# Moving two of eight streamed value tiles from a dense stage into a softmax wait

## The chip, the core and the metric

The kernel runs on one core of one Trainium2 chip. The metric is the device time of one execution in microseconds (us), the median over runs. Engines are named as in the profile: PE multiplies matrices, PEld is its weight load, DVE is the vector engine, ACT the scalar engine, POOL the general one, SP the queue that issues almost all transfers. Matmuls read SBUF and write PSUM, whose buffers are handed out by pools; a pool with one buffer gives the next tile the same place, so its writer has to wait until the tile before has been read.

## The reference

Two layers, each an attention block and a gated feed-forward block, are applied one after the other to four single-token sequences, with the same weights and the same caches in both layers:

```
def _A_ref(x, k_cache, v_cache, wq, wo):       # Hq 32, Hkv 8, Sk 4096, Dh 128
    q = (x @ wq) per head; k, v = caches, each kv head used by 4 query heads
    p = softmax(q k^T * Dh ** -0.5)
    return (p v) as [B, 1, 4096] @ wo
def _B_ref(x, w_gate, w_up, w_down):           # D 512, F 1792
    return (gelu(x @ w_gate) * (x @ w_up)) @ w_down

x = x + A(layernorm(x)); x = x + B(layernorm(x))
x = x + A(layernorm(x)); x = x + B(layernorm(x))
```

x is [4, 1, 512]; each cache is [4, 8, 4096, 128] in bf16, 32 MB. The caches are most of what has to be read, and the second layer needs them again.

## The kernel before, in words

**Tiling.** Batch b's keys and values are cut into tiles of 512 KB: a kv head has two (`NT` = 2) of 2048 positions each, on 128 partitions with 16 positions apiece. A head group has 4 kv heads (`GH`), so 8 tiles (`TG`); there are two groups. Keys stay in SBUF (`KP`) for both layers. Values go through a ring of 8 slots (`V_SLOTS`, class `VRing`, L607).

**Order of the work.** The order is written by hand: the kernel runs in a manual schedule, so each engine's queue holds its instructions in the order of the Python calls. The main loop runs over b. `attend_first` and the dense stage of b = 0 come first. Then, for each b, the dense stage of layer 1 is followed by the q rows of layer 2 and by `attend(b+1)`, which works on two batches at once: layer 2 of batch b and layer 1 of batch b+1. In `attend(b)`, `gx, gy` are the two groups; the scores of layer 2 (`sc2`) come first, with their softmaxes and the layer-2 values that are still in SBUF (`vals2`), then the scores of layer 1: group `gx`, softmax, group `gy`, softmax. DVE turns each key tile (L488, `turn`) before layer 1's scores use it. `vals1.step(n)` multiplies the next n value tiles. The first group's eight tiles are spent before and just behind the second group's softmax, the second group's eight after it, mixed with the output projection (`rows.heads`). The last three of these are kept in their slots for layer 2, and two are parked in PSUM by DVE (L500) and copied back by ACT later.

**The streamed tiles.** Eight layer-2 value tiles of batch b - 1, those of the group that layer 1 read first (`other2 = order[:TG]`), are loaded a second time. They are held back in `late2`, an object of `Streamed` (L794), which `attend` returns; the dense stage gets it as `prev`. `fill()` takes the next tile: `stream_v` (L692) multiplies it with the probabilities as weights, 8 matmuls of 32 x 256 into a PSUM tile `so`. `whole()` ends a pair of heads: DVE turns `so` (`turn_v`, L700), sums it (L707) and scales it (L708) into `OT2_bf`. In the kernel before, a pair of heads shares one `so` of 512 columns in the pool `ps_sc`, which has one buffer (tag "sc"); the scores use that same buffer, except for the first ones of each `attend`.

**Dense stage** (`dense`, from L1080; for b of 1 to 3 there are streamed tiles, for b = 0 `prev` does nothing). In order: `add_x`, a fill, the statistics, half of the gate matmuls, a fill (`halfway`), the other half; inside `gelu`, `up()` issues the up matmuls and two fills; then `gate_up` (L433), `whole()` for the first pair, the 56 down matmuls (`down_rows`, L273) and two fills. The main loop goes on with the q rows of layer 2, a fill behind `q_round`, a fill behind `q_build`, and `whole()` for the second pair. Eight fills in all.

**What sets the transfers.** SP runs its queue in order. `ring.extend` appends tiles to the ring's sequence; `ring.pump` (L617, the transfer itself L623) issues the next load for each free slot, at the point of the program where it is called. A load waits for the last reader of its slot, and whatever stands behind it on SP waits too. In `attend` the sequence is: `one(b)` (16 layer-1 tiles; for b of 2 and 3 the first two are loaded ahead), the 8 of `other2`, then the 3 of `own1`, which are layer-2 tiles for the next `attend`.

Of the kernel before, what the change touches and what calls it, by code (L numbers as in the profile page):

```python
# [8 lines left out]
FP32 = mybir.dt.float32  # L9
# [6 lines left out]
P = 128  # L16
# [18 lines left out]
def kernel(  # L35
# [15 lines left out]
    _, Hkv, Sk, Dh = A_k_cache.shape  # L51
# [8 lines left out]
    NT = C // CH  # L60
# [6 lines left out]
    TG = GH * NT  # L67
# [480 lines left out]
    def soft_turn(p0):  # L548
        flat = p0[0].rearrange("p c j -> p (c j)")
        nc.vector.transpose(out=flat, in_=flat)  # L550
# [32 lines left out]
    def one(b):  # L583
        return [(g * GH + s, t) for g in first_groups[b] for s in range(GH) for t in range(NT)]
# [113 lines left out]
    def turn_v(ps, n=1):  # L698
        flat = ps[:, :n * SW]
        nc.vector.transpose(out=flat, in_=flat)  # L700

    def sum_v(ps, out, rden, n=1):
        first = ps[:, :1]
        own = bass.AP(first.tensor, first.offset,
                      [list(first.ap[0]), [SW, n], [1, rep], [QS + rep, NW]])
        sums = ov[:, :n * rep].rearrange("p (k h) -> p k h", h=rep)
        nc.vector.tensor_reduce(out=sums, in_=own, axis=AX.X, op=ALU.add)  # L707
        nc.vector.tensor_tensor(out=out.rearrange("p (k h) -> p k h", h=rep), in0=sums, in1=rden,  # L708
                                op=ALU.mult)

    class Values:
# [8 lines left out]
        def fill(self, count):  # L720
            self.step(count, hold=True)
# [72 lines left out]
    class Streamed:  # L794
# [3 lines left out]
            self.b, self.tiles, self.prob, self.dst, self.n = b, tiles, prob, dst, 0  # L798
            self.sums = []

        def fill(self):
            kvh, t = self.tiles[self.n]
            self.n += 1
            g, s = divmod(kvh, GH)
            pe = self.prob[g][0]
            if t == 0 and s % 2 == 0:
                ps = ps_sc.tile([P, 2 * SW], FP32, name="so", tag="sc")
                self.sums.append((kvh, ps))
            ps = self.sums[-1][1]
            ring.pump()  # L810
            v, own = ring.ready.pop((2, self.b, kvh, t))
            at = s % 2 * SW
            stream_v(ps[:, at:at + SW], pe[:, s], v, t, t == 0, t == NT - 1)
            assert own
            ring.free.append(v)
            ring.pump()

        def whole(self):
            kvh, ps = self.sums.pop(0)
            g, s = divmod(kvh, GH)  # L820
            turn_v(ps, 2)
            sum_v(ps, self.dst(kvh, 2), self.prob[g][1][:, s:s + 2], 2)

    def dst1(b):
        last = one(b)[-1][0]
# [94 lines left out]
    def attend(b, qy, before, norm, early=None):  # L920

        gx, gy = second_groups[b - 1]
        prob1, prob2 = {}, {}
        keys, parked = early or (Keys(b, (gx, gy)), None)
        turn = keys.turn
        kept2, own2, other2, apart2 = two(b - 1)
        kept1, own1, _, apart1 = two(b)
        banks.late = len(apart2)
        vals2 = Values(2, b - 1, kept2 + own2 + apart2, prob2, dst2(b - 1),
                       off_ot=len(apart2) > 0)  # L930
        late2 = Streamed(b - 1, other2, prob2, dst2(b - 1))
        vals1 = Values(1, b, one(b), prob1, dst1(b), keeps=kept1,
                       streamed=[gy * GH + s for s in range(GH - 1)], park=apart1,
                       sums={4: (ps_sc, "sc"), 5: (ps_sm, "sm"), 6: (ps_sc, "sc")},
                       last_bank=lambda: ps_sm.tile([P, 2, WIDE], FP32, name="ot", tag="sm"))

        sc2 = [new_scores(early=True)]
        for t in range(NT):
            scores(sc2[0], gx, t)
            if parked and t == 0:  # L940
                freed = KP[gx][0][0]
                home = freed.rearrange("p h c d -> p (h c d)")
                parked.back(home, 2)
                KP[gx][0][0], KP[gy][NT - 1][1] = KP[gy][NT - 1][1], freed
                keys.load_pairs(GH // 2 - 1)
            else:
                keys.load_pairs(GH // 2)
        p0 = soft(sc2[0], norm)
        if parked:
            parked.back(home, 2)  # L950
        q_build(qy())
        sc2.append(new_scores())
        soft_turn(p0)
        ready = 2 if parked else 0
        turn(ready)
        for t in range(NT):
            scores(sc2[1], gy, t)
            keys.load(GH)
        ring.extend(1, b, one(b)[ahead_of[b]:])
        ring.extend(2, b - 1, other2)  # L960
        ring.extend(2, b, own1)
        pe0, den0 = soft_swap(p0, early=True), soft_den(p0)

        def recip():
            prob2[gx] = (pe0, soft_recip(den0))

        p1 = soft(sc2[1], norm, lasting=True, meanwhile=recip)
        vals2.step(2, hold=True)
        qe = q_sums(q1_bf[:, gx, :, b])
        vals2.step(4, hold=True)  # L970
        turn()
        soft_turn(p1)
        q_spread(qe)
        vals2.flush()
        turn(1 if ready else 2)
        pe1, den1 = soft_swap(p1, early=True), soft_den(p1)
        banks.back_brief()
        banks.back()
        turn()
        prob2[gy] = (pe1, soft_recip(den1))  # L980
        turn(0 if ready else 1)
        sc1 = new_scores()
        scores(sc1, gx, 0)
        turn(3)
        scores(sc1, gx, 1)
        turn()
        p0 = soft(sc1)
        vals2.step(vals2.left(), hold=True)
        turn()
        soft_turn(p0)  # L990
        q_build(q1_bf[:, gy, :, b])
        vals2.flush()
        pe, den = soft_swap(p0), soft_den(p0)
        turn()
        prob1[gx] = (pe, soft_recip(den))
        turn()
        vals1.step(2)
        sc1 = new_scores()
        scores(sc1, gy, 0)
        turn(4)  # L1000
        vals1.step(3)
        scores(sc1, gy, 1)
        p0 = soft(sc1)
        vals1.step(3)
        soft_turn(p0)
        heads = pairs(one(b))
        twice = o1(b)
        rows = RowProj(lambda i: twice(i).broadcast_to([P, 2]))
        prob1[gy] = (soft_swap(p0), soft_recip(soft_den(p0)))
        vals1.step(2)  # L1010
        rows.heads(heads[0], hp)
        vals1.step(2)
        rows.heads(heads[1], hp)
        vals1.step(1)
        rows.heads(heads[2], rep)
        vals1.step(1)
        rows.heads(heads[2] + rep, rep)
        rows.split()
        vals1.step(1)
        proj = OutProj(o1(b), 1)  # L1020
        proj.heads(heads[3], rep)
        vals1.step(1)
        assert vals1.left() == 0
        rows.onto(proj)
        proj.n = Hq - rep
        proj.heads(heads[3] + rep, rep)
        return proj.y, late2
# [52 lines left out]
    def dense(b0, nb, y, prev, scr):  # L1080
        first = b0 == 0 and nb == 1
        n = 2 * RUN if first else RUN

        def rhs(k):
            return xb[:, k, :n]

        def into(w_sb, name, halfway):
            if first:
                return ffn_in(rhs, w_sb, name, halfway)
            return ffn_rows(b0, w_sb, name, halfway)  # L1090

        def out_of(i, v):
            if not first:
                return turn_rows(v)
            nc.vector.tensor_scalar(out=cs_f[:, i], in0=v[:, :, B], scalar1=float(D), scalar2=None,
                                    op0=ALU.mult)
            return v[:, :, b0:b0 + nb]

        u = []

        def up():
            if first:
                busy(6)
            u.append(into(wu_sb, "u", None))
            if first:
                busy(4)
            else:
                for _ in range(2):
                    prev.fill()
                u[0] = out_of(1, u[0])  # L1110

        add_x(b0, nb, y)
        prev.fill()
        st = stats(b0, nb)
        add_y(b0, nb, y)
        rstd, mr = ln_scale(nb, st)
        t = [None if first else shifts(scr, mr, i) for i in range(2)]
        g = out_of(0, into(wg_sb, "g", prev.fill))
        sq = gelu(scr, g, shifts(scr, mr, 0) if first else t[0], rstd, up)
        uv = out_of(1, u[0]) if first else u[0]  # L1120
        H_bf = gate_up(scr, sq, uv, shifts(scr, mr, 1) if first else t[1], rstd)
        prev.whole()
        if first:
            y = down(nb, H_bf)
            busy(1)
            return y
        y = down_rows(H_bf)
        for _ in range(2):
            prev.fill()
        return turn_rows(y)  # L1130

    def dense_last(y, full):
# [167 lines left out]
```

## Time and profile before

| | |
|---|---|
| runs (3) | 273.52 us median, 272.98 to 275.62 |
| the profiled execution | 273.24 us, its span 271.5 us |
| PE busy | 180.9 us, 67% of the span, mean granted clock 0.843 |
| DVE busy | 176.3 us, 65% |
| ACT busy | 54.1 us, 20% |
| transfers | 103.08 MB, mean 380 GB/s |
| L488 DVE, turning keys | 74.1 us, 64 of 1208 ns |
| L692 PE, streamed values, 128x256 | 20.1 us in two groups, 400 matmuls |
| L759 PE, other values, 128x32 | 34.9 us, 1120 matmuls |

All durations used below come from the profiled execution, and times such as "125.59" are microseconds from the start of its span. "Busy" is summed over stages with different limits, so it does not tell which engine sets the end: that is read at each seam, from what a waiting instruction waits for. In a row of the timeline the numbers are start and length in us, then engine, line, operation, output<-inputs, shape and count, and in brackets the idle time before it with what ended that time. In a row of the chain of waits they are start, length, and what it was. In a table by stretches, each engine has its busy time with the number of instructions; the last three numbers are PE's granted clock, the share of the DMA engines and GB/s.

### The profile page before, as it was taken

Reading aid. Unit: us, or ns where it says so; the run is one execution under the profiler, and the core shown is the slowest. Engines: PE = TensorE matmul, PEld = TensorE weight load, DVE = VectorE, ACT = ScalarE, POOL = GpSimd, SP = SyncE. Lnnn points to the kernel's source line nnn. Section 1 sums busy time; section 2 is a strip of 40 time slices with the busy share of each in tenths; the row PEclk is TensorE's granted clock in tenths of the full one; section 3 lists DMA queues with packets and bytes.
Section 4 is the critical chain, followed back from the end, with each engine's and each line's share of the span. In section 5 each row is a group of like instructions: output and inputs, shape, how many; then the busy total and the mean of one; then the engine's idle time right before and its main releaser. Section 6 shows DMA issues by size and latency. Waiting matters only on the chain.

```text
span 271.5 us, 8960 instructions
## 1 busy us (share of the span) xinstructions
PE 180.9 (67%) x3982; PEld 110.6 (41%) x3982; DVE 176.3 (65%) x445; ACT 54.1 (20%) x113; POOL 2.7 (1%) x8
## 2 busy tenths in 40 slices
PE   1366254644696956868669458787596596977784
PEld 1313133533363524445327134454262253543463
DVE  3394951131224898875776989667759894877673
ACT  1001001100005402031023520310226102105630
POOL 2000000000000000000000000000000000000001
PEclk9999999555599795779997977799978556799999
DMA  7999999999984999999999999999999999999930
GB/s 250 422 416 421 416 421 416 410 383 406 407 325 147 405 415 419 418 418 416 416 404 407 417 420 417 417 416 388 381 421 418 416 423 414 369 383 378 415 132 3
DMA packets 32286, 103.08 MB, mean 380 GB/s; under 512 B 2676, under 2 KB 8568, under 8 KB 32248
## 3 DMA queue, kind: packets, MB, share of 16 engines
q1 hardware_dynamic: 32224, 102.51, 94.8%
q8 instruction: 31, 0.51, 0.7%
q14 instruction: 7, 0.06, 0.0%
q10 hardware_dynamic: 24, 0.01, 0.0%
HBM read 102.50 MB, written 0.00 MB: 378 GB/s over the span
## 4 chain that ended last, share of the span: by engine, by line
DMA 37%; DVE 28%; PE 23%; SPq 6%; issue 3%; ACT 1%; DVEq 0%
DMA v_t<-in_A_v_cache_dram 18%; DVE kp L488 16%; PE sc L521 10%; DMA kp<-in_A_k_cache_dram 9%; DMA wd_sb<-in_B_w_down_dram 6%; DMA kp<-in_A_v_cache_dram 4%; SPq L143 4%; PE ot L759 3%; PE so L692 2%; DVE pe L530 2%; DVE qb L313 2%; PE y L248 2%; PE q L273 1%; DVE q L280 1%; SPq L144 1%
## 5 line engine op out<-in xcount | busy, mean ns | idle before, releaser
L488 DVE STREAM_TRANSPOSE kp<-kp 128x1024 f32<-128x1024 f32 x64 | 74.1, 1208 | 0.0
L521 PE MATMUL sc<-kp,qb 128*32 128x512 bf16 x512 | 57.9, 492 | 20.7 <-DVE kp L488 15.2
L759 PE MATMUL ot<-pe,v_t 128*128 128x32 bf16 x1120 | 34.9, 182 | 13.0 <-DMA v_t<-in_A_v_cache_dram 11.6
L759 PEld LDWEIGHTS <-v_t 128*128 128x128 bf16 x1120 | 33.2, 101 | 23.8 <-DMA v_t<-in_A_v_cache_dram 13.8
L521 PEld LDWEIGHTS <-qb 128*32 128x32 bf16 x512 | 17.0, 106 | 48.6 <-issue 34.6
L542 ACT ACTIVATE pe<-sc,nl 128x512 bf16<-128x512 f32 x8 | 5.5, 687 | 88.8 <-DVE pe L539 61.8
L572 PE MATMUL x<-pe,ident_bf 128*32 128x128 bf16 x192 | 6.3, 262 | 16.5 <-DVE pe L550 16.5
L530 DVE TENSOR_REDUCE pe<-sc 128x1 f32<-128x512 f32 x12 | 8.3, 690 | 11.8 <-PE sc L521 11.8
L572 PEld LDWEIGHTS <-ident_bf 128*32 128x32 bf16 x256 | 5.9, 109 | 19.5 <-issue 18.2
L692 PE MATMUL so<-v_t,pl 128*32 128x256 bf16 x192 | 9.5, 275 | 3.6 <-DMA v_t<-in_A_v_cache_dram 3.4
L248 PE MATMUL y<-OT_bf,wo_sb 128*128 128x32 bf16 x192 | 7.3, 190 | 6.9 <-DMA wo_sb<-in_A_wo_dram 6.7
L248 PEld LDWEIGHTS <-wo_sb 128*128 128x128 bf16 x256 | 8.5, 102 | 8.1 <-DMA wo_sb<-in_A_wo_dram 7.1
L700 DVE STREAM_TRANSPOSE so<-so 128x256 f32<-128x256 f32 (+1 forms) x19 | 11.1, 583 | 1.0 <-PE so L692 0.9
L692 PE MATMUL so<-v_t,pe 128*32 128x256 bf16 x208 | 10.6, 338 | 1.2 <-ACT pe L575 1.1
L507 ACT COPY v_t<-park 128x1024 bf16<-128x1024 bf16 x12 | 11.3, 1031 | 0.0
L550 DVE STREAM_TRANSPOSE pe<-pe 128x512 bf16<-128x512 bf16 x12 | 8.4, 698 | 4.4 <-ACT pe L542 4.4
L370 DVE TENSOR_TENSOR xb<-XX,y 128x4 bf16<-128x4 f32 (+1 forms) x9 | 1.6, 174 | 14.5 <-PE y L248 14.4
L575 ACT CAST pe<-x 128x512 bf16<-128x512 f32 x12 | 7.0, 586 | 19.0 <-PE x L572 19.0
L605 DVE TENSOR_TENSOR OT_bf<-ot,rden 128x8 bf16<-128x8 f32 (+1 forms) x20 | 3.1, 157 | 10.7 <-PE ot L759 10.5
L351 PE MATMUL yr<-wo_sb,OT_bf 128*2 128x512 bf16 (+1 forms) x96 | 9.8, 478 | 0.1
L248 PE MATMUL q<-xb,wq_sb 128*128 128x5 bf16 (+1 forms) x192 | 5.5, 170 | 6.5 <-DMA wq_sb<-in_A_wq_dram 6.5
L307 PE MATMUL qe<-q_bf,ident_bf 128*32 128x16 bf16 x256 | 4.4, 176 | 8.0 <-DVE q_bf L296 6.1
(142 smaller groups left out, 217.3 us busy)
## 6 DMA issues: line engine op xcount, KB each, us to landing
v_t<-in_A_v_cache_dram SPq DMA_DIRECT2D x97, 512.0 KB, 8.4
kp<-in_A_k_cache_dram SPq DMA_DIRECT2D x40, 512.0 KB, 12.1
kp<-in_A_k_cache_dram SPq DMA_DIRECT2D x12, 1024.0 KB, 7.4
wq_sb<-in_A_wq_dram SPq DMA_DIRECT2D x2, 2048.0 KB, 14.7
wo_sb<-in_A_wo_dram SPq DMA_DIRECT2D x4, 1024.0 KB, 11.6
wq_sb<-in_A_v_cache_dram SPq DMA_DIRECT2D x2, 1024.0 KB, 10.8
wg_sb<-in_B_w_gate_dram SPq DMA_DIRECT2D x1, 1792.0 KB
wu_sb<-in_B_w_up_dram SPq DMA_DIRECT2D x1, 1792.0 KB
```

The costliest lines, as they stand in the source:

```text
L143: dq.dma_start(out=wo_sb[:, i * n:(i + 1) * n], in_=wo_dram[:, i * n:(i + 1) * n])
L248: nc.tensor.matmul(dst, lhsT=lhsT, rhs=rhs, start=first, stop=last, skip_group_check=True)
L351: nc.tensor.matmul(self.rows[j:j + x.shape[1]], lhsT=x, rhs=wo_sb[:, i], start=self.n < QD, stop=True, skip_group_check=True)
L488: nc.vector.transpose(out=words, in_=words)
L507: nc.scalar.copy(out=dst[:, i * n:(i + 1) * n], in_=self.parts[i])
L521: nc.tensor.matmul(sc[s * QS:(s + 1) * QS], lhsT=qb[:, w0:w0 + 2 * W], rhs=kt[:, :, be // 2, :, be % 2], start=(t == 0 and be == 0), stop= ...
L530: nc.vector.tensor_reduce(out=m, in_=sc.rearrange("p c j -> p (c j)"), axis=AX.X, op=ALU.min if norm else ALU.max)
L550: nc.vector.transpose(out=flat, in_=flat)
L572: nc.tensor.matmul(x[a * QS:(a + 1) * QS, s], lhsT=ident_bf[:, s * QS:(s + 1) * QS], rhs=pT[:, a], start=True, stop=True, skip_group_check ...
L692: nc.tensor.matmul(ps[d, :NW * QS], lhsT=x[:, w:w + NW].rearrange("p c h -> p (c h)"), rhs=v[:, i:i + NW, d], start=first and i == 0, stop ...
L700: nc.vector.transpose(out=flat, in_=flat)
L759: nc.tensor.matmul(self.ot[:, s % 2], lhsT=v[:, i, :], rhs=wide(pe[:, s, t * CH + i, :]), start=(done == 0 and i == 0), stop=(done == NT - ...
```

## The change

Two of the eight fills move from the dense stage into `attend`, behind the scores and the softmax of the second group and three value steps. Their head (the first of four) gets a PSUM tile of its own in the pool `ps_h`, and its own `whole()` before the reciprocal of that softmax. The second head now also has a tile of its own, in `ps_sc`; the third and fourth share one, as before. The dense stage loses the fill between the gate matmuls and one of the two behind the down matmuls; the two in `up()` stay. The ring's sequence changes with it: the two tiles are loaded between the layer-1 tiles of the first and of the second group.

```diff
@@ class Streamed
-        def fill(self):
+        def fill(self, early=False):
             kvh, t = self.tiles[self.n]
             self.n += 1
             g, s = divmod(kvh, GH)
             pe = self.prob[g][0]
-            if t == 0 and s % 2 == 0:
-                ps = ps_sc.tile([P, 2 * SW], FP32, name="so", tag="sc")
-                self.sums.append((kvh, ps))
-            ps = self.sums[-1][1]
+            alone = s < 2
+            if t == 0 and (alone or s % 2 == 0):
+                pool, tag = (ps_h, "h") if early else (ps_sc, "sc")
+                n = 1 if alone else 2
+                self.sums.append((kvh, n, pool.tile([P, n * SW], FP32, name="so", tag=tag)))
+            ps = self.sums[-1][2]
             ring.pump()
             v, own = ring.ready.pop((2, self.b, kvh, t))
-            at = s % 2 * SW
+            at = 0 if alone else s % 2 * SW
...
         def whole(self):
-            kvh, ps = self.sums.pop(0)
+            kvh, n, ps = self.sums.pop(0)
             g, s = divmod(kvh, GH)
-            turn_v(ps, 2)
-            sum_v(ps, self.dst(kvh, 2), self.prob[g][1][:, s:s + 2], 2)
+            turn_v(ps, n)
+            sum_v(ps, self.dst(kvh, n), self.prob[g][1][:, s:s + n], n)
@@ attend
-        ring.extend(1, b, one(b)[ahead_of[b]:])
-        ring.extend(2, b - 1, other2)
+        ring.extend(1, b, one(b)[ahead_of[b]:TG])
+        ring.extend(2, b - 1, other2[:NT])
+        ring.extend(1, b, one(b)[TG:])
+        ring.extend(2, b - 1, other2[NT:])
         ring.extend(2, b, own1)
...
         p0 = soft(sc1)
         vals1.step(3)
+        for _ in range(NT):
+            late2.fill(early=True)
         soft_turn(p0)
...
-        prob1[gy] = (soft_swap(p0), soft_recip(soft_den(p0)))
+        swapped, den = soft_swap(p0), soft_den(p0)
+        late2.whole()
+        prob1[gy] = (swapped, soft_recip(den))
@@ dense
-        g = out_of(0, into(wg_sb, "g", prev.fill))
+        g = out_of(0, into(wg_sb, "g", None))
...
         y = down_rows(H_bf)
-        for _ in range(2):
-            prev.fill()
+        prev.fill()
         return turn_rows(y)
```

## The prediction

> Names used here: A0 to A7 and B0 to B7 are the value tiles of layer 1's first and second head group in one attention pass, S0 to S7 the streamed second-layer tiles of `late2`. Pass b (1 to 3) is `attend(b)`; dense stage b follows it. Bm is the start of PE's last tile B7, which opens dense stage b.
>
> **What bounds the kernel now.** First the page: the digits of the DMA engines, the share of their queue, and the chain that ended last.
>
> ```profile
> DMA  7999999999984999999999999999999999999930
> q1 hardware_dynamic: 32224, 102.51, 94.8%
> DMA 37%; DVE 28%; PE 23%; SPq 6%; issue 3%; ACT 1%; DVEq 0%
> ```
>
> The transfers fill the span except for a dip near 82 us (before pass 1, which the edit does not touch). But they hold only 37% of the chain: DVE and PE together hold 51%. So two limits lie close together, and I ask at each seam which one ends last. The chain around dense stage 2 (start, length, what):
>
> ```profile
> 171.61 8.86 DMA v_t<-in_A_v_cache_dram
> 180.47 0.05 issue
> 180.51 0.58 PE ot L759 x16
> ...
> 182.27 6.15 DMA v_t<-in_A_v_cache_dram
> 188.42 0.04 issue
> 188.47 0.40 PE so L692 x8
> 188.87 0.89 PE q L273 x16
> ```
>
> B7 lands and PE starts it; later S5 lands and lets the q rows go, which stand behind S5 in PE's queue. Now the timeline of pass 1's end and dense stage 1:
>
> ```profile
> 118.22 0.41 PE L572 MATMUL x<-pe,ident_bf 128*32 128x128 bf16 x16 [1.86 <-DVE pe L550]
> ...
> 122.32 0.46 DVE L700 STREAM_TRANSPOSE so<-so 128x256 f32<-128x256 f32 x1
> ...
> 122.81 0.19 DVE L707 TENSOR_REDUCE ov<-so 128x4 f32<-128x32 f32 x1
> ...
> 124.34 0.57 PE L759 MATMUL ot<-pe,v_t 128*128 128x32 bf16 x16 [0.63 <-DMA v_t<-in_A_v_cache_dram]
> ...
> 125.59 0.57 PE L759 MATMUL ot<-pe,v_t 128*128 128x32 bf16 x16 [0.18 <-DMA v_t<-in_A_v_cache_dram]
> ...
> 131.53 0.22 DVE L433 TENSOR_TENSOR words<-words 128x56 bf16<-128x56 f32 x1
> 131.66 0.72 DVE L700 STREAM_TRANSPOSE so<-so 128x512 f32<-128x512 f32 x1
> 131.80 0.97 PE L273 MATMUL y<-wd_sb,words 128*32 128x128 bf16 x56 [0.83 <-DVE words L433]
> ```
>
> The first row is the wait that the change fills: PE idle 1.86 us until the softmax is turned. B6 and B7 both wait for their landing, 1.25 us apart: that is the time of one tile in the queue. The down projection starts 0.05 us after DVE's L433 ends (131.75): dense runs on DVE, and streamed tiles lie beside it. Pass 3 ends otherwise, and so does the kernel:
>
> ```profile
> 236.82 0.56 PE L759 MATMUL ot<-pe,v_t 128*128 128x32 bf16 x16
> ...
> 244.84 0.40 PE L692 MATMUL so<-v_t,pl 128*32 128x256 bf16 x8 [0.58 <-DMA v_t<-in_A_v_cache_dram]
> ```
> ```profile
> 261.90 0.57 PE L759 MATMUL ot<-pl,kp 128*128 128x32 bf16 x16 [0.41 <-DMA kp<-in_A_v_cache_dram]
> ```
>
> B7 of pass 3 waits for no DMA, and the kernel's last value tile waits only 0.41 us. From 125.59 on, a delay of the PE and DVE work thus reaches the end nearly whole.
>
> **The change, part by part.** *The queue's order.* S0 and S1 are now loaded ahead of B0. Eight slots rotate, so the first eight loads behind A go out when A0 to A7 are read, as before; the queue is full, and B7 lands two tiles later. Pass 1 waits for the queue at B6 and B7 already, so B1 goes from 125.59 to 128.09: **+2.50**. SP passes nothing else; the next two loads are freed by S0 and S1 themselves, not by parked B tiles, so they go out about 3 us earlier (120.49 before), which gives nothing while the queue is full.
>
> *The two early fills.* 2 x 8 matmuls, 0.40 us a tile at full clock (S rows of dense 1), 0.62 in pass 3 at half clock. PE's last A tile ends at 116.36, 171.48 and 228.11, the turned softmax arrives 1.8 us later: 2 x 0.62 fits. In pass 1, S1 lands only at about 118.1 (B1's old place), so the swap is some 0.3 us late; the 2.5 us of waiting above cover it. Without that cover it would cost 0.3. The small `whole` behind it on DVE (0.46 + 0.19 + 0.16, starts 0.49 and 0.23 apart: 0.88) lies in DVE's 0.82 us wait for `den`: nothing, at most 0.1 before the parks.
>
> *Dense without two fills.* The fill between the gate matmuls goes, but DVE's L390 and its turn of the gate follow the layer norm (128.91) as closely as the gate: nothing. S6 no longer stands ahead of the q rows, and S5, two places nearer its PE use, has landed: in stage 1 PE was ready as xb was (133.35, q at 133.41): nothing; in stage 2 xb is ready at 188.27, q starts 188.68: 0.41 less 0.06 of handover, **-0.35**; in stage 3, 244.51 and 245.06: **-0.49**.
>
> *The wait that the change adds.* Head 1 now has its sums alone, and `up()` still fills twice: S3, which ends head 1, and S4, which opens the pair of heads 2 and 3. That pair takes the same PSUM buffer (`ps_sc`, one buffer, tag "sc") that head 1 still occupies, and head 1 is read only by `whole()`, behind `gate_up` on DVE. The order of instructions shows S4's first weight load waiting on DVE, and the 56 down matmuls behind it in PE's queue. Cost in stage 1: turn starts 131.66, the reduction (last reader) 0.49 later and lasts 0.19: 132.34; PE starts S4 0.06 later (132.40), its eight matmuls give way after 0.35, down starts at 132.75 instead of 131.80: **+0.95**, in each of three stages. DVE is free when down ends, since `whole` has moved ahead of it. Bounds: nothing, if S4 does not wait after all (PE idles 0.83 us there now, and S4 has landed: first rival), and 1.15, if PE also waits for the product behind the reduction; I take 0.95, which the rows give for the last reader.
>
> *What the late fills free.* The load behind S4 goes out at the end of S4: stage 1, 7.25 us after the new B1, 135.34 instead of 133.15; its place at the DMA engines comes near 136.3. With an empty queue (84.19, first pair of keys) the trace's half-microsecond windows show 33, 123, 115 GB/s and only from 86.0 on over 300: 1.8 us to speed. So the queue idles some 0.8 us there, and 0.6 before the load behind S6: 1.4 at most, nothing at least if deeper overlap hides it. I take 1.0, nearer to the row. In pass 2 the two sides then meet: PE could have started B7 at about 180.05 (0.46 of waiting left out), + 2.50 + 0.95 = 183.50; the queue brings it at 180.47 + 2.50 + 1.0 = 183.97. So B2 is 184.0, **+3.5** (183.5 to 184.4).
>
> **Sum.** +3.5 at B2; stage 2 +0.95 - 0.35; pass 3 runs on PE and DVE and hands +4.1 on; stage 3 +0.95 - 0.49; the last 0.41 of waiting absorbs as much. 3.5 + 0.6 + 0.46 - 0.41 = +4.15. On the profiled execution's 273.24 (span 271.5): **277.4**, with the two ends of B2 276.9 and 277.8. The median of the runs, 273.52, is 0.28 above that execution, within its neighbours' spread (272.98 to 275.62).
>
> [...] The two passes differ:
>
> ```profile
> 136.40:180.00 43.60, 31.16 (x618) 18.01 (x619) 35.02 (x73) 11.61 (x23) 0.00 (x0) 0.84 1.03 415
> 191.70:236.80 45.10, 34.17 (x624) 19.16 (x625) 35.24 (x73) 11.61 (x22) 0.00 (x0) 0.70 1.02 409
> ```
>
> The same work took 1.5 us more where the granted clock (third number from the end) was 0.70. The clock was 0.50 at 60 to 64 us with PE busy all the time, and 1.00 at 140 to 142 with PE busy 0.48 of 2 us: in this trace more work does not release it. [...]
>
> **Rivals.**
> - *The bank wait stays off the path* (S4 gets in before `whole`, or down does not queue behind it). Then only the order counts: B1 +2.5, B2 at the queue's 182.97 (+2.46), -0.35, -0.49, -0.41: +1.2, **274.5**. For it: the fills of before lay wholly beside DVE. Against: one PE queue.
> - *Faster: the queue alone sets the end.* Between 188 and 196 and between 234 and 252 us it moves 330 to 390 GB/s instead of 420, together 2.9 us of lost transfer. Loads freed up to 4 us earlier by S0, S1 and the B tiles could close these dips: **270.3**. It decides if PE reaches B7 of pass 3 before its landing even 2.5 us later. Against: there PE waits for nothing now, and at the end only 0.41.
> - *The queue runs dry*: 3 us in each dense stage, twice my upper bound. B2 186.0; pass 3's B7 from the queue at 235.85 + 2.5 + 6.0 = 244.3, +7.5; with +0.46 and -0.41: **280.8**. Against: keys and loads have 5 to 10 us of lead after each stage.
> [...]
>
> **How the numbers follow.** My forecast 0.64; bank wait hidden 0.12; faster 0.04; queue dry 0.10; clock released 0.10. The range takes in the hidden bank wait and the fallen clock with the upper end of B2: 274.3 to 279.5; left out are the dry queue and the faster case, 0.14. About 1%, 2.7 us, is what a measurement of this kernel can tell from no change: slower (over 276.3) is 0.64 and 0.10 and a little of the clock case, 0.75; within 1% 0.21; faster 0.04.
>
> **What would show it.** B7 of pass 1 at about 128.1 and still waiting for DMA; the first matmul of S4 in each stage waiting for DVE L700 or L707, down 0.9 to 1.0 us later behind L433; no DMA wait left on S5; B7 of pass 3 near 241; the last value tile without a DMA wait. I am wrong if S4 starts before head 1's reduction, if B7 of pass 1 lands at its old time, or if PE of pass 3 waits at B7 for its landing.

## The result, and the profile after

The changed kernel takes **286.37 us** (median of 4 runs, 286.12 to 287.73), the kernel before in the same comparison 273.83 us (4 runs, 272.98 to 275.62). The ratio is 1.046 with a 95% interval of 1.040 to 1.052. The forecast was 277.4 us with a range up to 279.5: the sign was right, the size was three times too small (+4.15 forecast on the profiled execution, +12.9 measured). The profiled execution took 286.12 us, its span 284.3, the mean granted clock 0.793 (273.24, 271.5 and 0.843 before).

From the page of the changed kernel, the digits of the DMA engines and the shares of the chain that ended last:

```profile
DMA  7999999999929999999699999997899999987920
DMA 47%; PE 24%; DVE 19%; SPq 5%; issue 2%; ACT 2%; DVEq 0%; ACTq 0%
```

Before, the row of nines had one dip (near 82 us); now three new ones stand in it, near 135, 195 and 255 us, one for each dense stage. The transfers' share of the chain rose from 37% to 47%, and that of DVE fell from 28% to 19%. So the end is set by transfers more than before, although transfers have new holes: they came late. PE's timeline of the end of pass 1 and of dense stage 1 (start, length, engine, line, what, and in brackets the idle time before it and what ended that):

```profile
126.97 0.61 PE L759 MATMUL ot<-pe,v_t 128*128 128x32 bf16 x16 [0.52 <-DMA v_t<-in_A_v_cache_dram]
...
128.21 0.61 PE L759 MATMUL ot<-pe,v_t 128*128 128x32 bf16 x16
...
135.60 0.40 PE L692 MATMUL so<-v_t,pl 128*32 128x256 bf16 x8 [2.31 <-DVE ov L707]
135.83 1.66 PE L273 MATMUL y<-wd_sb,words 128*32 128x128 bf16 x56
...
138.13 1.60 PE L273 MATMUL q<-wq_sb,xb 128*32 128x512 bf16 x16 [0.21 <-DVE xb L370]
```

The second row is B7 of pass 1, at 128.21 instead of 125.59. The third is S4 behind PE's new wait for DVE's L707. The two rows behind it took 0.97 and 1.05 us before, and 1.66 and 1.60 now, with the same instructions. Now the chain of waits at the ends of passes 2 and 3 (start, length, what):

```profile
178.50 9.50 DMA v_t<-in_A_v_cache_dram
188.04 0.58 PE ot L759 x16
...
237.14 10.49 DMA v_t<-in_A_v_cache_dram
247.68 0.62 PE ot L759 x16
```

B7 of pass 2 starts when it lands, as before; B7 of pass 3 (247.68) now does so too, where it waited for no transfer before (236.82). In the same chain each of these two landings follows on one of the early tiles: S1 starts at 178.05 and 236.70, as it lands. And the stretches of dense stage 1 in the changed kernel (the last number of a row is GB/s, the third from the end PE's granted clock):

```profile
134.00:136.00 2.00, 0.40 (x19) 0.40 (x23) 1.57 (x9) 0.00 (x0) 0.00 (x0) 0.97 0.80 295
136.00:138.00 2.00, 1.92 (x65) 1.44 (x56) 0.43 (x2) 0.00 (x0) 0.00 (x0) 0.50 0.56 211
138.00:140.00 2.00, 1.87 (x28) 0.79 (x29) 0.45 (x3) 0.00 (x0) 0.00 (x0) 0.68 0.74 242
140.00:142.00 2.00, 1.04 (x40) 0.46 (x36) 1.79 (x9) 0.41 (x2) 0.00 (x0) 1.00 0.65 205
```

The same stage before moved 395 to 420 GB/s in every stretch of 2 us from 126 to 142. Against 419 GB/s (a tile of 512 KB in the 1.25 us between two landings) these four rows lose (124 + 208 + 177 + 214) / 419 x 2 us = 3.45 us of transfer, within 8 us.

The seams tell where the 12.9 us went. "Dense" is the time from B7 to the next layer's first scores, "pass" that from those scores to the next B7:

| part | before, us | after, us | difference | forecast |
|---|---|---|---|---|
| B7 of pass 1 (start) | 125.59 | 128.21 | +2.62 | +2.50 |
| dense 1 | 10.84 | 13.50 | +2.66 | +0.95 |
| pass 2 | 44.08 | 46.33 | +2.25 | +0.05 |
| dense 2 | 11.19 | 12.52 | +1.33 | +0.60 |
| pass 3 | 45.12 | 47.12 | +2.00 | 0 |
| dense 3 | 11.33 | 13.56 | +2.23 | +0.46 |
| from there to the end | 23.31 | 23.10 | -0.21 | -0.41 |

The first row is right within 0.12 us. All the rest came in parts that the forecast held to be small or nothing: the dense stages cost 6.2 instead of 2.0, passes 2 and 3 cost 4.25 instead of 0.05. Row by row, the 2.66 of dense 1 are 0.58 up to the end of L433 (the gate matmuls run at a granted clock of 0.50), 0.83 of wait, 0.69 in the down matmuls and 0.55 in the q rows. So 1.8 of them come with the low clock.

### The profile page after: what moved, and what is told of

Its sections match the earlier page's. It is cut to its first block, busy times and chain, and to the rows that moved or that the text cites. A ratio compares the mean times of both kernels' runs of the same rounds, so it can differ in the third digit from the quotient of the medians.

```text
span 284.3 us, 8962 instructions
## 1 busy us (share of the span) xinstructions
PE 186.9 (66%) x3978; PEld 113.1 (40%) x3982; DVE 177.6 (62%) x454; ACT 54.1 (19%) x113; POOL 2.7 (1%) x8
## 4 chain that ended last, share of the span: by engine, by line
DMA 47%; PE 24%; DVE 19%; SPq 5%; issue 2%; ACT 2%; DVEq 0%; ACTq 0%
DMA v_t<-in_A_v_cache_dram 31%; DMA kp<-in_A_k_cache_dram 11%; DVE kp L488 6%; PE sc L521 6%; DMA wu_sb<-in_B_w_up_dram 5%; PE ot L759 4%; SPq L143 4%; PE so L692 3%; PE q L273 2%; PE y L273 2%; PE y L248 1%; DVE pe L530 1%; DVE qb L313 1%; DVE q L280 1%; PE g L273 1%
## 5 line engine op out<-in xcount | busy, mean ns | idle before, releaser
L521 PE MATMUL sc<-kp,qb 128*32 128x512 bf16 x512 | 54.0, 462 | 18.3 <-DVE kp L488 13.5
L759 PE MATMUL ot<-pe,v_t 128*128 128x32 bf16 x1120 | 35.9, 183 | 15.9 <-DMA v_t<-in_A_v_cache_dram 13.5
L521 PEld LDWEIGHTS <-qb 128*32 128x32 bf16 x512 | 16.4, 102 | 44.7 <-issue 28.8
L692 PE MATMUL so<-v_t,pl 128*32 128x256 bf16 x192 | 11.0, 310 | 11.8 <-DVE ov L707 7.6
L700 DVE STREAM_TRANSPOSE so<-so 128x256 f32<-128x256 f32 (+1 forms) x22 | 11.7, 532 | 11.1 <-PE so L692 11.0
L692 PE MATMUL so<-v_t,pe 128*32 128x256 bf16 x208 | 12.7, 356 | 6.4 <-DMA v_t<-in_A_v_cache_dram 4.7
L351 PE MATMUL yr<-wo_sb,OT_bf 128*2 128x512 bf16 (+1 forms) x96 | 12.2, 569 | 0.0
L692 PEld LDWEIGHTS <-pe 128*32 128x32 bf16 x208 | 5.5, 105 | 14.7 <-issue 8.1
L692 PEld LDWEIGHTS <-pl 128*32 128x32 bf16 x240 | 5.4, 102 | 14.7 <-DVE ov L707 8.5
L572 PEld LDWEIGHTS <-ident_bf 128*32 128x32 bf16 x256 | 5.9, 105 | 13.0 <-issue 11.8
## 6 DMA issues: line engine op xcount, KB each, us to landing
wq_sb<-in_A_wq_dram SPq DMA_DIRECT2D x2, 2048.0 KB, 14.7
```

The costliest lines, as they stand in the source:

```text
L351: nc.tensor.matmul(self.rows[j:j + x.shape[1]], lhsT=x, rhs=wo_sb[:, i], start=self.n < QD, stop=True, skip_group_check=True)
L521: nc.tensor.matmul(sc[s * QS:(s + 1) * QS], lhsT=qb[:, w0:w0 + 2 * W], rhs=kt[:, :, be // 2, :, be % 2], start=(t == 0 and be == 0), stop= ...
L572: nc.tensor.matmul(x[a * QS:(a + 1) * QS, s], lhsT=ident_bf[:, s * QS:(s + 1) * QS], rhs=pT[:, a], start=True, stop=True, skip_group_check ...
L692: nc.tensor.matmul(ps[d, :NW * QS], lhsT=x[:, w:w + NW].rearrange("p c h -> p (c h)"), rhs=v[:, i:i + NW, d], start=first and i == 0, stop ...
L759: nc.tensor.matmul(self.ot[:, s % 2], lhsT=v[:, i, :], rhs=wide(pe[:, s, t * CH + i, :]), start=(done == 0 and i == 0), stop=(done == NT - ...
```

## The experiments

Two theories were put against each other first. One: PE's new wait for a PSUM bank, with what the clock does behind it, is what costs. The other: the order of the loads costs, since the two tiles loaded ahead leave the queue too little to move during the dense stage. Smaller parts (slots freed late, S5 behind the q rows, a busy PE in the softmax's wait) were then tried. Each run was compared with the kernel before, run in the same comparison; its medians there were 273.1 to 273.5 us.

**The changed kernel without the bank wait.** S4 goes behind the down matmuls, where DVE has read head 1's bank.

```diff
-                for _ in range(2):
-                    prev.fill()
+                prev.fill()
                 u[0] = out_of(1, u[0])
...
         y = down_rows(H_bf)
-        prev.fill()
+        for _ in range(2):
+            prev.fill()
```

> The changed kernel, but with one fill in up() and two behind the down matmuls, so that S4, the first fill that needs the PSUM buffer of head 1, stands behind the down matmuls. Queue order and early fills stay. Theory A (the bank wait is the seed: it holds the down matmuls, the idle PE is then given half clock for down and q, and the loads freed late let the transfer queue run dry, which passes 2 and 3 pay at S1 and B7): the down matmuls start within 0.1 us of L433's end and take 0.97 us again, dense stage 1 falls from 13.5 us to about 11.3, passes 2 and 3 lose most of their 2 us each, and the time comes to 275 to 278. Rival B (the order costs most: B7 lands two tiles later, and six fills free fewer loads): the bank wait is worth its own 0.83 us a stage, 2.5 in all, and the time stays at 283 or more.

Measured: 282.12 us, ratio 1.035 (1.027 to 1.043), span 280.3. That lies between the two expectations: 4.0 us of span come back, 8.8 stay. B7 starts at 128.24, 186.89 and 245.43; the dense stages are 12.71, 11.96 and 10.84 long. The first theory expected 0.97 us for the down matmuls again; that came only in stage 3. In stages 1 and 2 they took 1.68 and 1.69 us, though no PSUM bank was waited for. PE's timeline of stage 1:

```profile
135.26 1.68 PE L273 MATMUL y<-wd_sb,words 128*32 128x128 bf16 x56 [1.28 <-DVE words L433]
```

With fewer fills in front of the down matmuls, PE waits longer for L433 itself: 1.28 us here, 2.39 in stages 2 and 3, against 0.83, 0.30 and 1.25 in the kernel before. So neither theory carries the whole. What remains without the wait is the larger part, and it still has some half clock in it.

**The wait on the order of before.** Heads 0 and 1 each get a tile from the one buffer of `ps_sc`, all eight fills stay in the dense stage, and the loads keep their order. S2 and S3 in `up()` then wait for head 0's sums.

```diff
-            if t == 0 and s % 2 == 0:
-                ps = ps_sc.tile([P, 2 * SW], FP32, name="so", tag="sc")
+            alone = s < 2
+            if t == 0 and (alone or s % 2 == 0):
+                n = 1 if alone else 2
+                self.sums.append((kvh, n, ps_sc.tile([P, n * SW], FP32, name="so", tag="sc")))
...
         y = down_rows(H_bf)
+        prev.whole()
```

> The kernel before with its own order of loads and its eight fills, but with head 0 and head 1 each in a tile of its own in the same PSUM buffer: S2 in up() has to wait for the sums of head 0 behind gate_up, and S2 and S3 both stand ahead of the down matmuls. Theory A: the wait alone costs about 1.35 us a stage (0.6 until the reduction ends, 0.73 for two fills), with half clock and a drier queue 2 to 3.5 a stage: 280 to 284. Rival B (the order is the cause): 1.35 a stage, less 0.4 of waiting at S5 in stages 2 and 3: no more than 277.

Measured: 279.62 us, ratio 1.024 (1.018 to 1.031), span 276.5, 5.0 above before; just under the first theory's 280 to 284, above the second's 277. B7 of pass 1 is in its old place (125.45); the dense stages grew to 13.24, 11.88 and 13.06. PE's timeline of its stage 1:

```profile
132.37 0.91 PE L692 MATMUL so<-v_t,pl 128*32 128x256 bf16 x16 [2.81 <-DVE ov L707]
133.06 1.72 PE L273 MATMUL y<-wd_sb,words 128*32 128x128 bf16 x56
```

PE idles 2.81 us, and the down matmuls behind it take 1.72 us instead of 0.97. In stage 3 they took 1.71, in stage 2 they kept 0.95, behind a wait of the same 2.81 us. Two fills stand behind the wait here, one in the changed kernel, so this wait is some 0.4 us dearer (a fill took 0.40 us in S4's row of the changed kernel). Without the clock the stage would grow, by an estimate from the forecast's wait and that fill, by 0.95 + 0.4; stages 1 and 3 grew by 2.40 and 1.73, stage 2, which kept its clock, by 0.69.

**Matmuls in the wait.** The changed kernel, and seven more matmuls of 128x512 between S3 and S4, into a PSUM buffer of the statistics; nobody reads what they compute. The wait stays; PE is not idle in it.

```diff
+    def warm(count):
+        t = ps_sm.tile([P, 512], FP32, name="warm", tag="sm")
+        for _ in range(count):
+            nc.tensor.matmul(t[:], lhsT=ident_bf[:], rhs=wg_sb[:, 0, :512], start=True,
+                             stop=True, skip_group_check=True)
...
-                for _ in range(2):
-                    prev.fill()
+                prev.fill()
+                warm(7)
+                prev.fill()
```

> The changed kernel with seven matmuls of 128 x 512, whose result nobody reads, between S3 and S4 in up(), into the PSUM buffer of the statistics, which is free then: PE is busy during the bank wait instead of idle. [...] If half clock comes with much work, as the forecast read the trace, down stays at 1.66 and the time is 286 to 288 (at half clock the seven take 3 us, longer than the wait).

Measured: 283.05 us, ratio 1.036 (1.032 to 1.041), span 280.9, below the 286 to 288 expected for half clock that comes with much work. More work for PE made the kernel faster than the changed one: its four runs, 282.56 to 283.63, lie below all four of the changed kernel (another comparison, where before had 273.38 against 273.83). PE's timeline of its stage 1 (line numbers are 6 higher here, so L713 is L707 elsewhere):

```profile
135.80 0.40 PE L698 MATMUL so<-v_t,pl 128*32 128x256 bf16 x8 [0.61 <-DVE ov L713]
136.03 0.95 PE L273 MATMUL y<-wd_sb,words 128*32 128x128 bf16 x56
```

S4 starts as late as in the changed kernel (135.80 against 135.60), but down takes 0.95 instead of 1.66 us, in all three stages (0.95, 0.96, 0.96), and the q rows 1.05. Stage 2 shows it best: the changed kernel comes into it at 1.00 from 188 to 192, this one at 0.50 and 0.78, so a better start is not what keeps its clock. First the changed kernel, then this one, by stretches (PE's busy time is the first number behind the 2.00, the clock the third from the end):

```profile
192.00:194.00 2.00, 0.00 (x0) 0.00 (x0) 1.83 (x9) 0.21 (x1) 0.00 (x0) 0.98 1.02 414
194.00:196.00 2.00, 1.22 (x40) 1.12 (x44) 0.86 (x4) 0.00 (x0) 0.00 (x0) 0.50 0.70 281
```
```profile
192.00:194.00 2.00, 1.67 (x11) 0.58 (x7) 1.83 (x10) 0.21 (x1) 0.00 (x0) 1.00 0.77 262
194.00:196.00 2.00, 1.35 (x72) 1.12 (x72) 0.84 (x4) 0.00 (x0) 0.00 (x0) 1.00 0.50 199
```

Two microseconds without a matmul, and the next two are granted 0.50; with 1.67 us of matmuls in them, 1.00. The transfers did not recover (262 and 199 GB/s), so they are emptied by something else too.

**The order of loads alone.** The kernel before with nothing but the ring's sequence changed; all eight fills stay in the dense stage.

```diff
-        ring.extend(1, b, one(b)[ahead_of[b]:])
-        ring.extend(2, b - 1, other2)
+        ring.extend(1, b, one(b)[ahead_of[b]:TG])
+        ring.extend(2, b - 1, other2[:NT])
+        ring.extend(1, b, one(b)[TG:])
+        ring.extend(2, b - 1, other2[NT:])
```

> The kernel before with only the order of loads changed: S0 and S1 are loaded ahead of B0, but all eight fills stay where they were in the dense stage, and there is no bank wait. S0 and S1 hold two of the eight slots until then. Theory A: B7 of pass 1 lands 2.5 us later (about 128.1), dense finds S0 to S4 landed, and the time comes to 275 to 277. Rival B (the order costs most): loads behind B are freed later by two slots, passes 2 and 3 wait for DMA 2 us longer each, and the time is 280 or more.

Measured: 281.35 us, ratio 1.030 (1.023 to 1.036), span 280.7. B7 starts at 127.60, 185.91 and 244.58: +2.0, +5.4 and +7.8 to before. That is the second theory's 280 or more. Four lines that move no arithmetic cost about what the changed kernel costs without its bank wait (282.12). Nor is there a sign that the two early fills bring anything: the run without the bank wait has them, this one does not, and no gain can be told between 282.12 and 281.35.

**One tile ahead, and four.** The same edit with other sizes.

```diff
-        ring.extend(2, b - 1, other2[:NT])
+        ring.extend(2, b - 1, other2[:1])
...
-        ring.extend(2, b - 1, other2[NT:])
+        ring.extend(2, b - 1, other2[1:])
```

> As the run with the order alone, but only S0 is loaded ahead of B0; all eight fills stay in the dense stage. Theory C (between B7's landing and the first keys of the next pass the queue has a fixed number of tiles to move: 13 before, 11 with two tiles ahead; the dense stage lasts longer than 11 tiles of 1.25 us take, so each tile fewer leaves the queue empty for about as long, and the period of a pass is its 43 tiles plus that): B7 of pass 1 one tile later, about 126.5, half of the loss of the order alone, 276 to 279. Rival D (the loss comes from two slots held by S0 and S1 in the late pass, or from a threshold, not from the count): under 275, or as much as with two.

> As the run with the order alone, but S0 to S3 are loaded ahead of B0. Theory C: nine tiles are left behind B7, twice the loss of two tiles ahead: B7 of pass 1 at about 130.3, three stages of some 6 to 7 us lost transfer each, 287 to 292. Rival D: the late pass waits for slots, B7 lands later than 131 and the loss lies ahead of B7 instead of behind it; or little more than with two, 282 to 285.

Measured: one tile 278.0 us, ratio 1.014 (1.008 to 1.020), four tiles 297.5 us, ratio 1.088 (1.083 to 1.094). Over 0, 1, 2 and 4 tiles the spans of the profiled executions are 271.5, 276.7, 280.7 and 294.9: the cost grows with every tile. B7 of pass 1 moves to 125.59, 126.64, 127.60, 133.24: about 1 us for each up to two, a little under one tile's 1.25. With four it moves further, and the time lies above both expectations: four of the eight slots then hold tiles that are read only in the dense stage, SP issues no load between 127.5 and 135.30, and nothing moves from 134 to 136 (0 GB/s). So these runs change two things at once, the tiles left behind B7 and the slots that are free.

**Slots freed earlier.** The changed kernel with other pairs of heads (1 and 2 share a tile, 3 has its own), which removes the bank wait without a later S4, and with the fills at earlier places: one again between the gate matmuls, none behind `q_build`.

```diff
-            alone = s < 2
-            if t == 0 and (alone or s % 2 == 0):
+            alone = s in (0, 3)
+            if t == 0 and s != 2:
...
-            at = 0 if alone else s % 2 * SW
+            at = SW if s == 2 else 0
...
-        g = out_of(0, into(wg_sb, "g", None))
+        g = out_of(0, into(wg_sb, "g", prev.fill))
...
-            prev.fill()
             if b == B - 1:
```

> The changed kernel with its order of loads and its early fills, but the remaining heads paired otherwise: heads 1 and 2 share the PSUM tile, head 3 has its own. So no fill waits for a sum, and S2 to S5 stand where the kernel before had its first four fills (ahead of the statistics, between the gate matmuls, twice in up()); S6 stands behind down, S7 behind q_round, none behind q_build. The six loads behind B7 are freed as early as the dense stage can. Theory F (what empties the queue is when the slots are freed: in the changed kernel the second, third and fourth of the six are freed at 3.9 to 9 us behind B7, while the five tiles in flight last 6.2 us): lost transfer per stage falls from 3.6 to 5.8 us to about 1 to 1.5, the time to 275 to 277. Theory C in its strict form (two tiles fewer behind B7 are a lead of 2.5 us lost, whenever they are freed): 3 us lost a stage and 279 to 282.

Measured: 280.72 us, ratio 1.029 (1.025 to 1.033), span 278.2. No wait is left in `up()`, down takes 0.97 us in all stages, loads go out early, and still 7 us remain. That is in the 279 to 282 that the count of tiles alone let expect, and not in the 275 to 277 of late frees alone. Its stretches in and behind dense stage 1 (scores start at 139.67):

```profile
134.00:136.00 2.00, 0.97 (x60) 0.86 (x64) 1.83 (x9) 0.00 (x0) 0.00 (x0) 1.00 1.01 385
...
138.00:140.00 2.00, 0.81 (x32) 0.41 (x28) 1.79 (x9) 0.41 (x2) 0.00 (x0) 1.00 0.97 322
140.00:142.00 2.00, 2.00 (x44) 1.17 (x37) 0.91 (x4) 0.00 (x0) 0.00 (x0) 1.00 0.80 234
142.00:144.00 2.00, 0.52 (x12) 0.02 (x2) 1.86 (x7) 0.43 (x1) 0.00 (x0) 1.00 0.82 258
```

Where the changed kernel had 295 GB/s (134 to 136) this one has 385, at full clock; but it has 234 and 258 from 140 to 144. The hole begins some 4 us later. Earlier frees and the clock do not cure it.

**The late fill alone.** The kernel before, with S5's fill behind the q rows, so that they no longer wait for S5's landing (the forecast's gain of 0.35 and 0.49 us, without the rest).

```diff
         y = down_rows(H_bf)
-        for _ in range(2):
-            prev.fill()
+        prev.fill()
...
         raw = q_rows(b, gx) if b else None
+        if b:
+            prev.fill()
```

> The kernel before with one edit: S5, the second fill behind the down matmuls, stands behind the q rows of layer 2 instead of ahead of them, so that these do not wait for its landing. By the trace of before this frees 0.35 us in stage 2 and 0.49 in stage 3 on the chain of PE and DVE, and the load behind S5 goes out about 1 us later. Theory A and C: 0 to 0.8 us faster, 272.6 to 273.4 beside 273.4; if the queue behind S5 counts more, up to 1 us slower.

Measured: 276.49 us (12 runs, 272.68 to 277.78), ratio 1.007 (1.002 to 1.011). It is not faster, if anything slower. Its dense stages were 11.85, 10.87 and 12.09 us against 10.84, 11.19 and 11.33. In stages 1 and 3 its gate matmuls, which stand ahead of the edit, took 0.94 and 0.97 us instead of 0.56, as they did at a granted clock of 0.50 in the run with four tiles ahead (0.94 and 0.97). Why that came isn't settled; runs of this kernel and of before scatter over 5 us.

**Matmuls in the softmax's wait.** Six matmuls of 128x512 whose result nobody reads, where the change put its two fills: once on the kernel with the order alone, once on the kernel before.

```diff
         vals1.step(3)
+        warm = ps_h.tile([P, 512], FP32, name="warm", tag="h")
+        for _ in range(6):
+            nc.tensor.matmul(warm[:], lhsT=ident_bf[:], rhs=wg_sb[:, 0, :512], start=True,
+                             stop=True, skip_group_check=True)
         soft_turn(p0)
```

> The run with the order alone, plus six matmuls of 128 x 512 whose result nobody reads in the softmax wait of the second group (into a free PSUM buffer), so that PE is not idle 1.8 us there. In that run dense stage 1 started at half clock and lasted 11.85 instead of 10.84 us. Theory C (the count of tiles behind B7 sets the loss): if the clock is full at the start of the dense stages they last 10.8 to 11.2 us, the loss of transfer falls by no more than that, and the time comes to 278 to 281. Rival E (the clock is the cause, the order only lowers PE's work before dense): with dense at 10.8 the loss behind B7 goes and the time is under 276.

> The kernel before, plus the same six matmuls in the same softmax wait. At full clock they take 1.3 us and fit into 1.86 us; at half clock 2.6 us, 0.7 more than the wait, as in pass 3 of the profiled execution. If half clock at the start of a dense stage is what spreads the runs of before (271.8 to 276.8), the median falls to about 272; if the clock does not follow this wait, the time is 273 to 275.

Measured: 282.0 us, ratio 1.031 (1.024 to 1.038), on the order alone (281.35 without), and 274.79 us (12 runs), ratio 1.004 (1.000 to 1.008), on the kernel before. Filling this wait gains nothing in either. In the first, dense stage 2 was 10.77 us long, shorter than before's 11.19, and from B7 of pass 2 to B7 of pass 3 it still took 58.65 us (186.99 to 245.64) against 56.31. So slow dense stages alone do not cause that lateness.

None of the ten beat the kernel before.

## Why the forecast was right in sign and wrong in size

**The queue's order, +2.50 at B7 of pass 1: right.** It is 128.21 (forecast 128.09), and it is still paced by the landings: B6 waits 0.52 us for its own, and B7 follows 1.24 us later.

**Where the bank wait lies, and its own length: right.** The row of S4 names DVE's L707, as forecast, and the down matmuls stand behind it in all three stages. From the end of L433 on DVE (134.95, 194.13, 254.41) to the start of down it takes 0.88, 1.05 and 0.88 us. The forecast had 1.00: its +0.95 and the 0.05 of before.

**Dense without two fills: right where it can be seen.** The q rows wait for DVE's `xb` alone, no longer for S5. In the run without the bank wait dense stage 3 is 10.84, which is before's 11.33 less the forecast's 0.49. Tried alone, this was no gain.

**"What the late fills free", taken as 1.0 us with 1.4 as its bound, and only in stage 1: this term of the sum failed, by its size and by being counted once.** Over each dense stage and the 8 us behind it, the packets of the trace give the transfer time lost against 419 GB/s:

| kernel | stage 1 | stage 2 | stage 3 |
|---|---|---|---|
| before | 0.5 | 1.1 | 1.5 |
| after | 5.8 | 4.5 | 5.2 |
| order alone | 3.9 | 4.4 | 3.6 |
| order, early fills, no bank wait | 4.5 | 4.0 | 3.6 |
| slots freed earlier | 2.7 | 4.3 | 2.7 |

The forecast looked at when two of the slots are freed and priced one short hole behind each. It did not follow the queue through the stage, nor count how many tiles it still holds when B7 lands. SP's timeline, before and then after (start, length, line, how many issues):

```profile
111.92 24.56 SPq L623 DMA_DIRECT2D v_t<-in_A_v_cache_dram  x19
137.55 2.17 SPq L481 DMA_DIRECT2D kp<-in_A_k_cache_dram  x4
```
```profile
112.33 29.43 SPq L623 DMA_DIRECT2D v_t<-in_A_v_cache_dram  x17
142.80 2.04 SPq L481 DMA_DIRECT2D kp<-in_A_k_cache_dram  x4
```

The next pass's first keys can go out only 1.1 us behind its first scores (136.43 and 141.71), so all that the queue has to move from B7's landing until then is what the sequence holds behind B7. In stages 1 and 2 of before, these are S0 to S7, three tiles of `own1` and two loaded ahead: 13 tiles, at 1.25 us each 16.25 us. With S0 and S1 loaded earlier they are 11, 13.75 us. A dense stage of 10.8 to 11.8 us, 1.1 us to the issue and the 1.8 us to speed that the forecast read at 84.19 make 13.7 to 14.7: 16.25 covers that, 13.75 hardly or not. So the 2.5 us at B7 of pass 1 were not only a delay that later parts could hide: they came out of the queue's lead, and each dense stage loses transfer again.

That count is only part of it. From B7 of pass 1 to the first keys the kernel before moved 9.4 of its 13 tiles in 12.0 us (412 GB/s); the changed kernel moved 8.6 of its 11 in 14.6 us (309 GB/s), and the order alone, where S0 and S1 hold two slots until the dense stage, 7.5 of 11 in 13.0 us (304 GB/s). In these two it was not the tiles that had run out: the loads left late, since each waits for a fill to free its slot. SP issued the changed kernel's last six at 130.27, 133.34, 136.05, 137.95, 140.29 and 141.43, up to 3.1 us apart; the eight of before left between 127.35 and 136.15, 0.4 to 2.1 us apart. With slots freed earlier 9.4 of 11 were moved in 12.9 us (380 GB/s), and there the hole lies from 140 to 144 us, about where 11 tiles from 127.88 end (141.6); that run still loses 2.7 to 4.3 us a stage. So fewer tiles behind B7 is the likely account for what stays there, and late loads come on top in the changed kernel. That is worked out; the count was not tried by itself. Its step fits only roughly: two tiles are 2.5 us, while the order alone loses 3.4, 3.3 and 2.1 us a stage more than before. Its level does not: the sum above leaves the kernel before 1.5 to 2.5 us to spare, yet it loses 0.5 to 1.5.

**"Pass 3 runs on PE and DVE and hands +4.1 on": failed with it.** B7 of pass 3 starts as it lands (the chain's 237.14 and 247.68), which the forecast had named as what would prove it wrong. From B7 to B7 the changed kernel takes 59.83 and 59.64 us. The 22.60 and 23.08 MB that it moves in them take 53.9 and 55.1 us at 419 GB/s, and 5.9 and 4.55 are lost: together 59.8 and 59.65. So both passes go by the transfers; before they took 54.92 and 56.31. The rival "the queue runs dry" had this mechanism, a chance of 0.10 and 280.8 us; the profiled executions took 286.12 us and, without the bank wait, 282.09. The forecast held a lead of 5 to 10 us against it; when the first keys of pass 2 went out, 2.4 of the 11 tiles were left to move, 3.0 us at its own 1.25 a tile (3.6 tiles and 4.5 us before).

**The clock: a row was misread, and the cost lay in another place.** The forecast read from this trace that more work does not release the clock, with 0.50 at 60 to 64 us "with PE busy all the time" as its first row. The row does not say that. PE was busy 1.18 us of each 2, and it waited 1.52 us for `wo_sb` ahead of each group of matmuls:

```profile
60.00:62.00 2.00, 1.18 (x32) 1.07 (x32) 0.00 (x0) 0.00 (x0) 0.00 (x0) 0.50 1.08 385
120.00:122.00 2.00, 2.00 (x36) 1.15 (x32) 1.98 (x4) 0.00 (x0) 0.00 (x0) 0.50 1.03 422
122.00:124.00 2.00, 1.71 (x36) 0.66 (x24) 1.54 (x6) 0.19 (x1) 0.00 (x0) 0.88 1.03 420
```

In the second row, also of before, PE is busy all the time, and in the third the clock comes back to 0.88. So the first row does not show that more work leaves the clock down. The forecast's other row, 1.00 at 140 to 142 with PE busy 0.48 us, was read rightly, but the next two microseconds are granted only 0.74. The forecast then gave the bank wait no cost beyond its length, and weighed the clock only in passes 2 and 3. The upper end of its range and one of its chances hold a clock that falls or is released there; no run shows what that is worth by itself. In the changed kernel the granted clock was 0.71 in pass 2 (141.71 to 188.04) and 0.72 in pass 3 (200.56 to 247.68), against 0.84 and 0.70 in the forecast's rows of before, and both passes went by the transfers. Part of what the low clock cost came where the change made PE idle, ahead of the down matmuls: 2.31 and 2.99 us of waiting are followed by a granted clock of 0.50 (136 to 138 and 194 to 196 us), and with seven matmuls in that wait it stays at 1.00. A wait of this length does not always do it: of eight waits of 2.31 to 2.99 us ahead of the down matmuls (three in the changed kernel, two without the bank wait, three with the wait on the order of before), six had half clock behind them (the down matmuls took 1.66 to 1.72 us) and two, of 2.39 and 2.81 us, had not (0.97 and 0.95 us).

The seven matmuls took 3.4 us off the span, nearly as much as taking the bank wait away (4.0). What the wait is worth by itself, at full clock, these two runs do not show: the one without the wait still has two down projections at half clock.

**The early fills.** The swap of pass 1 comes on time (118.23 against 118.22, where 0.3 late was feared). In passes 2 and 3 PE waits 0.90 and 0.82 us for S1's landing just ahead of it, so there the early tiles are themselves waited for. No gain is to be seen: B7 is paced by the landings in every pass, so time won ahead of it is waited away.

Put together on the span: 8.8 stay without the bank wait (order, late transfers, and half clock in two stages), taking the wait away gives back 4.0, together 12.8, the difference of the spans. The order alone gives 9.2 in its own profiled execution. The parts are single executions of kernels whose runs differ by 2 to 4 us, so the split is good to about 2 us.

**What stays open.** How the transfer lost in a stage divides between fewer tiles behind B7 and loads that leave late: the run with slots freed earlier keeps the count but drops the bank wait too, and no run changes the count alone. The clock in dense stage 1 of the changed kernel is already at half speed from about 119 us on, where before had 1.00 from 124 on. The rows show PE busy 2.00 of 2 us from 120 to 122 before, and 1.54 after, with waits of 0.5 us for landings at 120.46 and 122.92; that these waits are the reason was not tried.

## What to carry to other kernels

When a load is moved ahead in a full queue, count what is left behind it: how many tiles the queue can still move before the next loads may be issued, when each of them gets a free slot, and whether they last as long as the work in between. A delay of a full queue is paid once only if the queue stays full; where it then runs dry, each later round pays (with the order alone, 2.0 us at B7 of pass 1, and then 3.4, 3.3 and 2.1 us of transfer a stage lost beyond what before loses). And price a new wait of PE with the clock behind it as well as with its length (behind the waits of 2.31 to 2.99 us in the changed kernel the down matmuls took 1.66 to 1.71 us instead of 0.96 to 0.97). Where the wait cannot be avoided, put something PE may do into it (seven matmuls took 3.4 us off the span here).

## What the runs showed of the hardware

More matmuls made a kernel faster: seven of 128x512, 1.69 us in all, in PE's wait of 2.3 to 3 us took 3.4 us off the span (down 0.95 instead of 1.66 to 1.71 us). But a PE that was mostly busy stayed at half clock: in the changed kernel, the stretches of 2 us from 120 to 132 have 1.54, 1.44, 1.89, 1.49, 1.73 and 2.00 us of PE work, 84%, all at 0.50. Up to 129 us PE has gaps of 0.1 to 0.6 us there, and no stretch without one is longer than 2.4 us (122.92 to 125.30); from 129.09 to 133.29 it has none, and S3, at 132.90, is the first tile to take 0.39 us again instead of 0.62. Whether the gaps are what kept the clock down was not tried.
